# Delta-rule attention and Fourier mixing: combined operands for the first batch, the second weight converted later, constants loaded ahead of memsets

## The chip, the cores and the metric

The kernel runs on one core of one Trainium2 chip. The metric is the device time of one execution in microseconds (us). TensorE (PE in the profile) multiplies matrices, VectorE (DVE) and ScalarE (ACT) do elementwise work, GpSimd (POOL) does a little of it and starts some DMAs, and SyncE (SP) starts most of the DMAs. PEld is TensorE's loading of the stationary operand.

## The reference

The first block is a delta-rule attention with 4 batches, 8 heads, 768 steps and head size 48. The second mixes its output with a two-dimensional Fourier transform, normalises it and sends it through two weight matrices.

```python
# attention, per batch and head
k_n = k / (norm(k) + 1e-6)
for t in range(S):
    y[t] = q[t] @ state
    v_old = state.T @ k_n[t]
    state = state + beta[t] * outer(k_n[t], v[t] - v_old)
# bridge: (B, H, S, D) -> x of (B, S, H*D) = (4, 768, 384)
mixed = real(fft(fft(x, axis=1), axis=2))
u = x + mixed
un = (u - mean(u)) / sqrt(var(u) + 1e-6)
out = u + relu(un @ w_ch1) @ w_ch2          # 384 -> 1536 -> 384
```

Queries, keys, values and beta come as 32-bit floats. The two weights come as 64-bit floats, so the kernel has to make 32-bit words of them itself.

## The kernel before

**Chunks.** The sequence is cut into chunks of 64 steps, 12 a batch and 48 in all; four chunks form a quad, two quads a group. Write K, Q and V for the keys, queries and values of a chunk, S for the state ahead of it, B for beta and the norms, and T for the inverse of a unit triangular 64x64 matrix made of K K^T and B. Then the chunk's contribution is U = T B (V − K S), the next state is S + K^T U, and the output is Q S plus a masked (Q K^T) U. Only S runs from chunk to chunk; everything else can be made ahead.

**Making ahead.** `prepare` (L342 and on) transposes keys and queries on TensorE (`pt`), copies them into the tile KQT (L374, L378, L379), forms the products K K^T and K Q^T (`pg`), copies the first into A (L405, L407) and masks the second into LQ (L410). `squares` (L335, L336) and `norms_of` (L427 to L438) give the norms of the keys. `invert(g)` works on a whole group of two quads: 30 steps of two VectorE instructions each (L463, L465), transposes on VectorE (L448, L472, L474), and two small rounds of matmuls (`pj`) by which the 64x64 inverses come together in the tiles wt (L496 to L500); wt holds T B transposed. `scaled` (L185) scales the values.

**The chain.** `chain(m)` issues chunk m: `pk` = K S on TensorE, R = V − pk on VectorE (L537), `pu` = T B R on TensorE, a copy of it into U on ScalarE (L546), `pS` = K^T U on TensorE, and two sums on VectorE that give the next state (L563). `pk`, `pu` and `pS` all lie in one PSUM tile, which the profile calls pc. `outputs` adds the two parts of the output in `py` and copies them into x (L583), in halves that the next chunk's chain carries along. At the start of each quad, chain asks for more keys, queries and values (SP's DMAs, L156).

**The rest of the work.** When a batch's chunks are done, `second` runs `fourier` on its x (VectorE sums and differences into the scratch tile scr from L624 on, matmuls `pf` and `pb`, sums into x, L660, statistics, L689) and then `mlp`, which takes two row tiles at a time: normalise and transpose (L706, `ptr`, L711), twelve blocks of three matmuls against w1 (`ph`, L723), then the products with w2 (`po`), and the last sum and the store (L736). The tile hT between the two weights has one buffer. A last row group of a batch is left for the batch after it.

**The weights.** `weights` reads each 64-bit weight as pairs of words through a staging tile, in 24 passes: ScalarE makes two pieces (L288, L290), VectorE puts the sign in (L306), shifts (L309) and adds (L312). Each pass uses one of two temporaries, on the tags F and scr, which `fourier` uses too.

**The order.** Each helper is a generator that gives up control after a piece. The loop at the end of the kernel takes the chunks in order and, at each of the three points where `chain` gives up control, advances the work ahead (`pre`) and the work on the side (`side`) by 2.4 pieces each; during the first eight chunks `side` advances only when `pre` is done. `side` is first the weights, and from chunk 12 on, after what is left of the weights has been run, `second` of the batch before. At every eighth chunk what is left of `pre` is run. A planner then places each engine's instructions, in the main by this order, and may move ready instructions ahead of waiting ones[...].

**The start.** POOL first clears tiles (L133), then starts the DMAs for the packed constants (`pack`, which holds the identity for the transposes, L192), beta (`bt`, L194, in a tile on the tag F) and the first key and value rows (L196, L197). The first matmuls are those that turn beta by chunk (`psb`, L124), whose copy is bcol (L224), and after them come the transposes of `keys(0)`.

Of the kernel before, what the change touches and what calls it, by code (L numbers as in the profile page):

```python
# [17 lines left out]
CH = 64  # L18
# [64 lines left out]
def kernel(  # L83
# [46 lines left out]

    def zeroed(shape, name, eng, part=lambda t: t):
        t = const.tile(shape, F32, name=name)
        eng.memset(part(t), 0.0)  # L133
        return t
# [53 lines left out]
    pack = const.tile([128, 128 + CH + NBH + 2], F32, name="pack")  # L188
    bt = wk.tile([NBH, S], F32, tag="F", name="bt")
    k0 = const.tile([NBH, D], F32, name="k0")  # L190
    v0 = const.tile([NBH, D], F32, name="v0")
    nc.gpsimd.dma_start(out=pack, in_=cn["pack"].ap())  # L192
    load(0, 0, (nc.sync, nc.scalar))
    nc.gpsimd.dma_start(out=bt, in_=beta.rearrange("b h s -> (b h) s"))  # L194
    load(1, 0, (nc.sync, nc.scalar))
    nc.gpsimd.dma_start(out=k0, in_=k.rearrange("b h s d -> (b h) s d")[:, 0, :])  # L196
    nc.gpsimd.dma_start(out=v0, in_=v.rearrange("b h s d -> (b h) s d")[:, 0, :])  # L197
# [18 lines left out]


    psb = ps_one([128, NCH, NBH // 2], "psb")
    for n in range(NCH):
        for hh in range(2):  # L220
            t0 = CH * n + (1 if n < NCH // 2 else 0)
            mm(psb[64 * hh:64 * hh + 64, n, :], bt[:, t0:t0 + CH], sel[:, hh, :], n == 0)
    bcol = const.tile([128, B * NQ, QT * 4], F32, name="bcol")
    nc.vector.tensor_copy(bcol.rearrange("p (b i) (c u) -> p b (i c) u", b=B, u=4),  # L224
                          psb.rearrange("p n (b u) -> p b n u", b=B))
    nl = NCH // 2 - 1
    twice = bcol[:, :, 4 * (nl % QT):4 * (nl % QT) + 4].rearrange(
        "p (b i) u -> p b i u", b=B)[:, :, nl // QT]
    nc.vector.tensor_scalar(twice, twice, once, None, op0=ALU.mult)
# [21 lines left out]
    def weights():  # L251

        if moe_w_ch1.dtype == F32:
            nc.sync.dma_start(out=w1, in_=moe_w_ch1.rearrange("(c p) f -> p c f", p=128))
            nc.sync.dma_start(out=w2, in_=moe_w_ch2.rearrange("(c p) m -> p c m", p=128))
            return
        w1v = moe_w_ch1.bitcast(I32).rearrange("(c p) (f two) -> p c f two", p=128, two=2)
        w2v = moe_w_ch2.bitcast(I32).rearrange("(c p) (m two) -> p c m two", p=128, two=2)  # L260
        nw = DFF // 2
        halves = [(w1v[:, i, a * nw:a * nw + nw], w1[:, i, a * nw:a * nw + nw])
                  for i in range(KD) for a in range(2)]
        n2 = nw // DM
        halves += [(w2v[:, i:i + n2], w2[:, i:i + n2]) for i in range(0, KF, n2)]
        stage = wk.tile([128, 2, nw, 2], I32, tag="hT", name="w64")

        def fetched(i):
            if i < len(halves):
                src, t = halves[i][0], stage[:, i % 2]  # L270
                if len(src.shape) == 4:
                    t = t.rearrange("p (c m) two -> p c m two", c=src.shape[1])
                nc.sync.dma_start(out=t, in_=src)

        np_ = nw // 2
        tmps = [wk.tile([128, 2, np_], I32, tag=tag, name="wtmp") for tag in ("F", "scr")]

        def words(p):
            cs = slice(p % 2 * np_, (p % 2 + 1) * np_)
            return stage[:, p // 2 % 2, cs, 0], stage[:, p // 2 % 2, cs, 1], tmps[p % 2]  # L280

        def first(p):

            lo, hi, t = words(p)
            tc.keep_in_program_order(nc.scalar.activation(  # L288
                t[:, 0], lo.bitcast(mybir.dt.uint32), ACT.Copy, scale=2.0 ** -29))
            tc.keep_in_program_order(nc.scalar.activation(  # L290
                t[:, 1].bitcast(F32), hi.bitcast(F32), ACT.Abs, scale=2.0 ** -112))

        fetched(0)
        fetched(1)
        yield
        first(0)
        for p in range(2 * len(halves)):
            lo, hi, t = words(p)
            dst = halves[p // 2][1]
            if len(dst.shape) == 3:  # L300
                dst = dst.rearrange("p c m -> p (c m)")
            dst = dst[:, p % 2 * np_:(p % 2 + 1) * np_].bitcast(I32)
            low, mag = t[:, 0], t[:, 1]
            if p + 1 < 2 * len(halves):
                first(p + 1)
            tc.keep_in_program_order(nc.vector.scalar_tensor_tensor(  # L306
                low, hi, -2 ** 31, low, op0=ALU.bitwise_and, op1=ALU.bitwise_or))
            yield
            tc.keep_in_program_order(nc.vector.tensor_scalar(  # L309
                mag, mag, 3, None, op0=ALU.logical_shift_left))  # L310
            u16 = mybir.dt.uint16
            nc.vector._custom_dve(dve_ops.ADD32_U16LIMBS, out=dst.bitcast(u16),  # L312
                                  in0=mag.bitcast(u16), in1=low.bitcast(u16))
            if p % 2:
                fetched(p // 2 + 2)
            yield
# [21 lines left out]
    def prepare(Q, parts=(0, 1)):  # L338
# [4 lines left out]
        a0, na = parts[0], len(parts)  # L343
        g, lh = divmod(Q, 2)
        if 0 in parts:
# [7 lines left out]
            if Q == NB:  # L353
                KQT = xbufs[2].rearrange("p t d -> p (t d)")[:, 0:QT * 8 * CH].rearrange(
                    "p (c j h a t) -> p c j h a t", c=QT, j=2, h=2, a=2)
            else:
                KQT = wk.tile([128, QT, 2, 2, 2, CH], F32, tag="KQT", bufs=NB, name="KQT")
# [5 lines left out]
        for c2 in range(QT // 2):  # L363
            for c in (2 * c2, 2 * c2 + 1):
                pt = ps_one([128, na, 2, 2, CH], "pt")
                for a in parts:
                    for j in range(2):
                        tr(pt[:, a - a0, j].rearrange("p h t -> p (h t)"),
                           (kp, qp)[a][:, c, 2 * j:2 * j + 2, :].rearrange("p u d -> p (u d)"),
                           a == a0 and j == 0)  # L370
                dst = KQT[:, c, :, :, a0:a0 + na].rearrange("p j h a t -> p a (j h) t")
# [3 lines left out]
                else:  # L375

                    if na == 2:
                        nc.scalar.activation(dst[:, 0], src[:, 0], ACT.Copy)  # L378
                    nc.scalar.activation(dst[:, na - 1], src[:, na - 1, :, ::-1], ACT.Copy)  # L379
# [124 lines left out]

    def chain(m):
# [29 lines left out]
        R = wk.tile([128, 4, D], F32, tag="R", name="R")  # L535
        ue = "p (j e) d -> p e j d"
        nc.vector.tensor_tensor(R.rearrange(ue, e=2), V4[:, c].rearrange(ue, e=2), pk, op=ALU.subtract)  # L537
        yield from advancing(later)

        pu = pc[:, 0, 4 * D:8 * D].rearrange("p (u d) -> p u d", u=4)  # L540
        for u in range(4):
            for hh in range(2):
                pr = slice(64 * hh, 64 * hh + 64)
                mm(pu[pr, u], wt[pr, c, u], R[pr, u], True)
        U = wk.tile([128, 4, D], F32, tag="U", bufs=2, name="U")
        nc.scalar.activation(U, pu, ACT.Copy)  # L546
# [226 lines left out]
    def second(b):  # L773
# [5 lines left out]
        else:  # L779
            yield from fourier(b)  # L780
        yield from mlp(b, list(range(TH if b == B - 1 else TH - 1)))
# [16 lines left out]
    side = weights()  # L798
    advance(side)
    run(keys(0))  # L800
    load(2, 0)
# [10 lines left out]
    scaled(0)  # L812
    pre = both(invert(1), queries(2, 3))
    due = [0.0, 0.0]
    for m in range(STEPS):
        b, n = divmod(m, NCH)
        if m % (2 * QT) == 0 and m > 0:
# [3 lines left out]
            due = [0.0, 0.0]  # L821
        for i, _ in enumerate(chain(m)):
# [51 lines left out]
```

## Time and profile before

| | |
|---|---|
| median of 6 runs | 832.75 us (824.89 to 837.65) |
| profiled execution | 835.15 us |
| its span, first to last instruction | 833.4 us |
| PE busy | 739.7 us, 89% of the span |
| weight load busy | 548.4 us, 66% |
| DVE busy | 398.2 us, 48% |
| ACT busy | 286.0 us, 34% |
| mean granted TensorE clock | 0.903 |
| start of the first Fourier mixing (L624) | 166.9 us |
| start of the first `ph` | 204.5 us |

An instruction's line in the profile is its line in the kernel file; nearly all matmuls come from one helper (L124) and are told apart by the tile that they write. A 32-bit matmul appears as two records for one call in the source, a transpose as one. The durations and idle times are of one execution. The granted clock is the part of full speed that TensorE was given.

### The profile page before, as it was taken

To read this page: it belongs to the slowest core of one execution; us is meant where nothing else is said; L and a number is where in the kernel's file an instruction comes from. 1 tells how busy PE (TensorE), PEld (TensorE's weight loads), DVE (VectorE), ACT (ScalarE), POOL (GpSimd) and SP (SyncE) were. 2 spreads that over 40 slices of the span, in tenths; PEclk is the share of its full clock that TensorE was granted. 3 is DMA by queue.
4 is the path that set the end of the run, shared out by engine and by line. 5 is a ranking of instruction groups with operands and counts; after the bars stand their busy time and mean duration, and the time that the engine had idled before them with its cause. 6 is when DMAs were issued, how large, how long until landed. Compare 5 with 4: busy or idle time off the path is not lost.

```text
span 833.4 us, 18790 instructions
## 1 busy us (share of the span) xinstructions
PE 739.7 (89%) x8024; PEld 548.4 (66%) x8024; DVE 398.2 (48%) x1036; ACT 286.0 (34%) x667; POOL 45.8 (5%) x67
## 2 busy tenths in 40 slices
PE   4768776785999987889999999999899989999997
PEld 3537565674767666665766766766667667676784
DVE  5985968859951146981169313499110124310000
ACT  5725258532273141371431632511521113030120
POOL 3000000011000000010000001000000010000000
PEclk9985955577999996999999699999699999999999
DMA  7542326610111121101102001001000000000000
GB/s 156 119 102 44 62 40 191 181 20 15 26 30 24 36 40 24 20 13 35 28 18 46 2 11 30 1 2 39 2 2 20 2 20 1 9 10 20 9 10 19
DMA packets 84051, 30.81 MB, mean 37 GB/s; under 512 B 79248, under 2 KB 80784, under 8 KB 83968
## 3 DMA queue, kind: packets, MB, share of 16 engines
q1 hardware_dynamic: 80880, 26.63, 14.6%
q0 software_dynamic: 912, 2.59, 0.9%
q8 instruction: 63, 1.03, 0.5%
q10 hardware_dynamic: 2176, 0.39, 0.3%
q14 instruction: 20, 0.16, 0.1%
HBM read 24.87 MB, written 4.72 MB: 36 GB/s over the span
## 4 chain that ended last, share of the span: by engine, by line
PE 70%; DVE 12%; ACT 11%; DMA 3%; issue 3%; SPq 1%; POOL 1%; POOLq 0%; ACTq 0%; DVEq 0%
PE ph L124 22%; PE po L124 21%; PE pc L124 7%; PE py L124 6%; PE pg L124 3%; PE pf L124 3%; PE pj L124 2%; PE pb L124 2%; PE pt L127 2%; DMA w<-in_moe_w_ch_dram 2%; ACT A L407 2%; DVE X L465 1%; ACT wt L497 1%; DVE A L463 1%; DMA kp<-in_k_dram 1%
## 5 line engine op out<-in xcount | busy, mean ns | idle before, releaser
L124 PE MATMUL ph<-unT,w 128*128 128x256 f32 x864 | 222.4, 406 | 6.2 <-ACT hT L723 2.9
L124 PE MATMUL po<-w,hT 128*128 128x384 f32 x576 | 200.3, 495 | 0.0
L124 PEld LDWEIGHTS ph<-unT,w 128*128 128x128 f32 x864 | 164.6, 199 | 37.4 <-ACT hT L723 6.1
L124 PEld LDWEIGHTS po<-w,hT 128*128 128x128 f32 x576 | 105.1, 190 | 65.3 <-issue 0.5
L723 ACT ACTIVATE hT<-ph 128x256 f32<-128x256 f32 x144 | 55.0, 383 | 208.8 <-PE ph L124 208.5
L563 DVE TENSOR_TENSOR st<-st,pc 48x192 f32<-48x192 f32 x88 | 30.9, 351 | 95.8 <-PE pc L124 63.0
L736 DVE TENSOR_TENSOR x<-x,po 128x384 f32<-128x384 f32 x24 | 13.3, 554 | 126.6 <-PE po L124 126.5
L546 ACT ACTIVATE U<-pc 128x192 f32<-128x192 f32 x48 | 15.8, 330 | 120.7 <-PE pc L124 115.7
L124 PE MATMUL pc<-R,wt 64*64 64x48 f32 x768 | 42.4, 249 | 12.3 <-DVE R L537 7.1
L124 PEld LDWEIGHTS pc<-R,wt 64*64 64x64 f32 x768 | 34.3, 160 | 28.0 <-DVE R L537 9.0
L463 DVE TENSOR_TENSOR A<-X 128x30 f32<-128x30 f32 (+9 forms) x150 | 50.6, 337 | 3.8
L465 DVE TENSOR_TENSOR X<-X,A 128x30 f32<-128x30 f32 (+9 forms) x150 | 49.3, 328 | 3.7
L124 PE MATMUL py<-st,KQT 128*64 128x96 f32 x352 | 44.9, 275 | 1.2 <-ACT x L583 1.2
L407 ACT ACTIVATE A<-pg 32x256 f32<-32x256 f32 x108 | 36.6, 369 | 18.4 <-PE pg L124 17.7
L124 PE MATMUL pg<-KQT 48*64 48x128 f32 (+1 forms) x896 | 35.8, 306 | 6.8 <-ACT w L407 2.3
L124 PE MATMUL py<-U,LQ 64*64 64x48 f32 x768 | 40.7, 240 | 0.0
L124 PEld LDWEIGHTS pg<-KQT 48*64 48x64 f32 x896 | 27.8, 173 | 17.8 <-ACT KQT L374 4.7
L124 PEld LDWEIGHTS py<-st,KQT 128*64 128x64 f32 x352 | 34.8, 152 | 5.9 <-ACT x L583 1.9
L124 PEld LDWEIGHTS py<-U,LQ 64*64 64x64 f32 x768 | 34.6, 154 | 2.2 <-issue 1.2
L660 DVE TENSOR_TENSOR x<-x,pb 128x193 f32<-128x193 f32 (+1 forms) x96 | 27.1, 345 | 18.3 <-PE pb L124 18.3
L124 PE MATMUL pf<-stab,scr 128*128 128x128 f32 (+6 forms) x192 | 27.6, 294 | 9.1 <-DVE scr L634 8.9
L583 ACT ACTIVATE x<-py 64x384 f32<-64x384 f32 x44 | 21.3, 484 | 38.5 <-PE py L124 37.1
(127 smaller groups left out, 811.5 us busy)
## 6 DMA issues: line engine op xcount, KB each, us to landing
w<-in_moe_w_ch_dram SPq DMA_DIRECT2D x12, 768.0 KB, 5.2
qp<-in_q_dram SPq DMA_DIRECT2D x96, 48.0 KB, 2.6
V<-in_v_dram SPq DMA_DIRECT2D x96, 48.0 KB, 2.5
kp<-in_k_dram SPq DMA_DIRECT2D x88, 48.0 KB, 2.4
out_dram<-x SPq DMA_DIRECT2D x8, 192.0 KB, 1.9
out_dram<-x SPq DMA_DIRECT2D x4, 168.0 KB, 2.1
stab<-k_stab SPq DMA_DIRECT2D x1, 640.5 KB, 4.3
kp<-in_k_dram ACTq DMA_DIRECT2D x8, 48.0 KB, 3.4
```

What stands on the lines that cost most here:

```text
L124: nc.tensor.matmul(o, lhsT=lhsT, rhs=rhs, start=start, stop=stop, skip_group_check=True)
L127: nc.tensor.matmul(o, lhsT=src, rhs=ident[0:src.shape[0], 0:src.shape[0]], is_transpose=True, start=start, stop=True, skip_group_check=True)
L407: nc.scalar.activation(ce(A[pr, ns, :, sl]), src, ACT.Copy)
L463: nc.vector.tensor_tensor(t, X[:, j:j + 1, j + 1:].broadcast_to([128, j, n]), X[:, 0:j, j:j + 1].broadcast_to([128, j, n]), op=ALU.mult)
L465: nc.vector.tensor_tensor(X[:, 0:j, j + 1:], X[:, 0:j, j + 1:], t, op=ALU.add)
L497: nc.scalar.activation(wt[r1, :, :, 0:W], Z[r1, ns], ACT.Copy)
L546: nc.scalar.activation(U, pu, ACT.Copy)
L563: nc.vector.tensor_tensor(nst[pr, :, :, e, :], st[pr, :, :, e, :], pS[pr], op=ALU.add)
L583: nc.scalar.activation(xs[b][yr, T].rearrange("p (h u d) -> p h u d", h=2, u=4), py[yr], ACT.Copy, scale=live[yr] if n == NCH // 2 - 1 els ...
L660: nc.vector.tensor_tensor(dst, dst, src, op=op)
L723: nc.scalar.activation(hT[:, fc, :], ph, ACT.Relu)
L736: nc.vector.tensor_tensor(x[:, T, :], x[:, T, :], po, op=ALU.add)
```

## The change

Three things change.

First, in batch 0 (chunks 0 to 11) the chain no longer multiplies by T B. A new function, `combined(m)`, forms T B K transposed (`pm`) and T B V (`pv`) for a chunk and writes them over the keys in KQT and over the values. The chain's R is then U itself. `combined` is called two chunks ahead inside the chain; for chunks 0, 1, 8 and 9 it is called in front of the chain. Because quad 3 belongs to batch 1 and its KQT lay in a buffer that now has another use, its keys are transposed once more into a usual KQT tile together with its queries.

Second, `weights` takes a part. Part 0, the first weight, stands where both stood. Part 1, the second weight, is staged in the third x buffer in three slots; its first fetches start at chunk 12, and its twelve passes come one behind each of the first `ph` blocks of batch 0.

Third, the four POOL DMAs for constants, beta and first rows are issued ahead of the tile clearing, and the beta matmuls move behind `keys(0)`.

```diff
+    pack = const.tile([128, 128 + CH + NBH + 2], F32, name="pack")
+    bt = wk.tile([NBH, S], F32, tag="F", name="bt")
...
+    nc.gpsimd.dma_start(out=pack, in_=cn["pack"].ap())
+    nc.gpsimd.dma_start(out=bt, in_=beta.rearrange("b h s -> (b h) s"))
+    nc.gpsimd.dma_start(out=k0, in_=k.rearrange("b h s d -> (b h) s d")[:, 0, :])
+    nc.gpsimd.dma_start(out=v0, in_=v.rearrange("b h s d -> (b h) s d")[:, 0, :])
...
     def zeroed(shape, name, eng, part=lambda t: t):
...
-    psb = ps_one([128, NCH, NBH // 2], "psb")
-    for n in range(NCH):
...
+    def betas():
+
+        psb = ps_one([128, NCH, NBH // 2], "psb")
...
-    def weights():
+    def weights(part):
...
-        stage = wk.tile([128, 2, nw, 2], I32, tag="hT", name="w64")
+        np_ = nw // 2
+        if part == 0:
+            halves = [(w1v[:, i, a * nw:a * nw + nw], w1[:, i, a * nw:a * nw + nw])
+                      for i in range(KD) for a in range(2)]
+            n, stage = 2, wk.tile([128, 2, nw, 2], I32, tag="hT", name="w64")
+        else:
+            halves = [(w2v[:, i, a * np_:a * np_ + np_], w2[:, i, a * np_:a * np_ + np_])
+                      for i in range(KF) for a in range(DM // np_)]
+            n, stage = 1, xbufs[2].rearrange("p t d -> p (t d)")[:, 0:6 * np_].bitcast(I32).rearrange(
+                "p (i f two) -> p i f two", i=3, two=2)
+        ns = stage.shape[1]
...
-        fetched(0)
-        fetched(1)
-        yield
+        for i in range(ns):
+            fetched(i)
+        yield
+        tmps = [wk.tile([128, 2, np_], I32, tag=tag, name="wtmp") for tag in ("F", "scr")]
         first(0)
...
+        again = Q == NB and parts == (1,)
+        taken = (0, 1) if again else parts
...
             if Q == NB:
-                KQT = xbufs[2].rearrange("p t d -> p (t d)")[:, 0:QT * 8 * CH].rearrange(
+                KQT = w2.rearrange("p c m -> p (c m)")[:, 2048:2048 + QT * 8 * CH].rearrange(
                     "p (c j h a t) -> p c j h a t", c=QT, j=2, h=2, a=2)
-            else:
-                KQT = wk.tile([128, QT, 2, 2, 2, CH], F32, tag="KQT", bufs=NB, name="KQT")
+        if Q != NB and 0 in parts or again:
+            KQT = wk.tile([128, QT, 2, 2, 2, CH], F32, tag="KQT", bufs=NB, name="KQT")
...
+    def combined(m):
+
+
+        Q, c = divmod(m, QT)
+        KQT, kp, _ = held[Q]
+        wt = wts[Q % NB]
+        scaled(Q)
+        pm = ps_pair("pm", "pair")[:, :, 0:2 * CH].rearrange("p h (j t) -> p h j t", j=2)
+        for j in range(2):
+            for hh, e in ((0, 0), (1, 1), (0, 1), (1, 0)):
+                pr = slice(64 * hh, 64 * hh + 64)
+                mm(pm[64 * e:64 * e + 64, hh, j], kp[pr, c, 2 * j + e, :], wt[pr, c, 2 * j + e], j == 0)
+        nc.scalar.activation(KQT[:, c, :, :, 0, :].rearrange("p j h t -> p h j t"), pm, ACT.Copy)
+        pv = ps_one([128, 4, D], "pv")
+        for u in range(4):
+            for hh in range(2):
+                pr = slice(64 * hh, 64 * hh + 64)
+                mm(pv[pr, u], wt[pr, c, u], vals[Q][pr, c, u], True)
+        nc.scalar.activation(vals[Q][:, c], pv, ACT.Copy)
+
     def chain(m):
...
-        R = wk.tile([128, 4, D], F32, tag="R", name="R")
+        if m < NCH:
+            U = R = wk.tile([128, 4, D], F32, tag="U", bufs=2, name="U")
+        else:
+            R = wk.tile([128, 4, D], F32, tag="R", name="R")
...
+        if m < NCH:
+            if (m + 2) % (2 * QT) > 1 and m + 2 < NCH:
+                combined(m + 2)
+        else:
+
+            pu = pc[:, 0, 4 * D:8 * D].rearrange("p (u d) -> p u d", u=4)
...
         else:
+            w = weights(1)
+            advance(w)
             yield from fourier(b)
-        yield from mlp(b, list(range(TH if b == B - 1 else TH - 1)))
+        channels = mlp(b, list(range(TH if b == B - 1 else TH - 1)))
+        if b == 0:
+            for _ in range(KF + 1):
+                advance(channels)
+                advance(w, 2)
+                yield
+            run(w)
+        yield from channels
...
-    side = weights()
+    side = weights(0)
     advance(side)
     run(keys(0))
+    betas()
...
-    scaled(0)
+    combined(0)
+    combined(1)
     pre = both(invert(1), queries(2, 3))
...
+            for i in (m, m + 1):
+                if i < NCH:
+                    combined(i)
```

## The prediction

> **What bounds the kernel now.** The profiled execution took 835.15 us for a span of 833.4 us. I read the busy time of each engine by stage first (columns: stretch in us, its length, busy us and instruction count of PE, weight load, DVE, ACT, POOL, granted TensorE clock, DMA share, GB/s).
>
> ```profile
> 0.00:69.30 69.30, 43.10 (x654) 31.25 (x654) 50.84 (x139) 38.77 (x94) 9.78 (x19) 0.92 0.56 119
> 69.30:121.30 52.00, 41.88 (x948) 35.79 (x948) 39.58 (x98) 18.51 (x39) 0.00 (x0) 0.70 0.28 46
> 121.30:158.00 36.70, 25.80 (x492) 22.63 (x494) 29.80 (x70) 27.95 (x63) 0.00 (x0) 0.50 0.61 184
> 158.00:167.00 9.00, 7.86 (x126) 6.94 (x124) 7.60 (x25) 4.57 (x12) 0.00 (x0) 0.50 0.53 133
> 167.00:204.50 37.50, 26.29 (x255) 20.74 (x251) 28.03 (x80) 12.17 (x31) 6.77 (x9) 0.77 0.11 19
> 204.50:233.00 28.50, 28.12 (x236) 21.76 (x235) 26.32 (x65) 7.88 (x19) 0.00 (x0) 0.94 0.11 19
> 250.00:302.00 52.00, 52.00 (x493) 36.52 (x488) 7.05 (x17) 13.03 (x34) 1.53 (x2) 1.00 0.15 30
> ```
>
> From 204.5 us, where the first channel matmuls (ph) begin, to the end PE is busy 594.8 of 628.9 us: that part is PE's, and the change adds no matmul to it. Before it PE is busy 144.9 of 204.5 us, half of the time at half clock. So the change is worth what it moves the start of ph, less what it stalls PE afterwards.
>
> What fixes the start of ph? The time order of DVE and ACT around 160 us (start, duration, instruction):
>
> ```profile
> 157.54 0.48 ACT L583 ACTIVATE x<-py 64x384 f32<-64x384 f32 x1 [1.62 <-PE py L124]
> ...
> 164.20 0.55 DVE L306 SCALAR_TENSOR_TENSOR wtmp<-w,wtmp 128x384 int32<-128x384 int32 x1
> 164.67 0.35 DVE L309 TENSOR_SCALAR wtmp<-wtmp 128x384 int32<-128x384 int32 x1
> ...
> 165.06 0.56 DVE L312 CUSTOM_DVE_ANT_0 w<-wtmp 128x768 uint16<-128x768 uint16 x1
> 166.66 0.35 DVE L563 TENSOR_TENSOR st<-st,pc 48x192 f32<-48x192 f32 x1 [1.05 <-PE pc L124]
> 166.94 1.34 DVE L624 TENSOR_TENSOR scr<-x 128x1152 f32<-128x1152 f32 x1
> ```
>
> The last output of batch 0 is in x at 158.0; the Fourier mixing (L624) begins only at 166.9, behind the weight conversion, which ends at 165.6 and also holds the scratch buffers (tags F and scr). The sizes, from the groups:
>
> ```profile
> L312 DVE CUSTOM_DVE_ANT_0 w<-wtmp 128x768 uint16<-128x768 uint16 x24 | 13.6, 566 | 0.2
> L306 DVE SCALAR_TENSOR_TENSOR wtmp<-w,wtmp 128x384 int32<-128x384 int32 x24 | 13.3, 553 | 5.7 <-ACT wtmp L288 5.5
> L288 ACT ACTIVATE wtmp<-w 128x384 int32<-128x384 uint32 x24 | 13.1, 544 | 3.4 <-DMA w<-in_moe_w_ch_dram 2.5 <-DVE w L312 0.7
> L290 ACT ACTIVATE wtmp<-w 128x384 f32<-128x384 f32 x24 | 12.9, 539 | 0.0
> L546 ACT ACTIVATE U<-pc 128x192 f32<-128x192 f32 x48 | 15.8, 330 | 120.7 <-PE pc L124 115.7
> ```
>
> **The change, part by part.** One conversion pass is .553 + .353 (L309) + .566 = 1.47 us of DVE and 1.08 of ACT. By the starts of L306, 3 of the 24 passes run before 121.3, 17 from there to 158.0 and 4 after.
>
> *Second weight moved.* 12 passes (17.7 us DVE, 13.0 us ACT) leave the front. The other 12 keep their place: 3 early, 9 after 121.3. So the stretch 121.3–158.0 loses 8 passes: DVE 29.8 − 11.8 = 18.0, ACT 27.95 − 8.6 = 19.3. The 9.0 us behind it (4 passes) stops standing between x and L624.
>
> *Combined operands.* Per chunk of batch 0, 8 source matmuls (pu; 16 records) and the copy U (.33) go; 8 for pm, 8 for pv (32 records), a copy into KQT (128x256, .38 as L374 and L379 take) and one into V (128x192, .33) come. Sixteen pc<-R records took 1.09 us at half clock (154.12) and .67 at full clock (88.55). Pm's 64 columns I put at 1.2 or .75; so a chunk costs PE 1.2 or .75 us more. Here the Trainium skill (TensorE: Matmul & The Clock Gate, table "Why this matters for your kernels") speaks of the clock: without idle gaps over about 3 us TensorE should keep full speed. The trace disagrees: from 145.0 to 177.2 us the granted clock is half, though no PE gap exceeds 1.5 us. By the rule the stretch 121.3–158.0 would hold about (25.8 + 4.8) × .62 = 19 us of PE work; by the row, 25.8 + 4 × 1.2 = 30.6 us. I take the row. That makes PE the largest sum there (DVE 18.0, ACT 19.3 + 4 × .38 = 20.8), and with 2.4 us of dependency gaps (10.9 us of PE idle there today, most of it behind conversion instructions) it becomes 33.0 us: 3.7 earlier. Together with the 9.0 us: 12.7 us for the start of L624.
>
> In 69.3–121.3 the shorter chain buys little. One step there takes PE .45 + .87 + .67 + .40 + .65 = 3.0 us at full clock and recurs after 4.2 to 5.0 (R at 83.96, 88.12, 93.14, 97.65), while invert(1) keeps DVE at 17.0 of 20 us in 80–100. The wait R→pu→U goes (about .9 us a step beyond PE's work), .75 of PE work comes; the end of invert(1), which gives wt of quad 2, is set by DVE. At chunk 0 the combination is serial behind wt (pm, copy, pk, R instead of pu, U: +2 us). The repeated K transposes of quad 3 are 8 records of about .3 us, 2.4 us of PE, among PE idle of 10 us. Bounds: 2 us earlier, 4 later; I take 0, the value of the DVE row.
>
> *Constants first.* Pack's DMA is issued at 4.18, behind 3.5 us of POOL memsets; psb waits until 8.82 for beta and holds the first transposes until 11.5. Key data were there at 6.5. The first KQT copy (12.22) may come 1 to 3 us sooner; ACT's table loads and squares (to 10.95) hold it. Against this, psb's 2.7 us of PE comes after keys(0), and the temporary on tag F, which bt occupies, is free later: passes 0 and 1 slide from 18–23 us toward invert(0), which starts at 26.4; at worst their 2.9 us of DVE are lost there. Bounds: 2.5 gain, 2 loss; I take 1 us gain, nearest to ACT's 10.95 against 12.22.
>
> *What becomes late next.* Chunks 12 and 13, done beside the last passes today, now lie beside the mixing. 167.0–204.5 has PE 26.3 and DVE 28.0 of 37.5 us; 7.9 us of PE and 7.6 − 5.9 = 1.7 of DVE join. It fits; bounds 0 and 7, I take 2 us lost.
>
> *Where the second weight lands.* Thirteen side steps of the first group: each has one ph block (6 records, 1.54 us), one pass, one step of invert(2) (.66) and .15 of the chain on DVE: 2.28 us of DVE against about 1.96 of PE (with the chain). Twelve passes end after 27 us; po begins after about 24 us and wants its last piece of w2 some 7 us later, so po itself isn't held. But DVE stands at 26.3 of 28.5 us in 204.5–233, so invert(2) ends up to 17.7 us later, and wt of quad 4 with it (238.4 today). PE can go on with po (about 17 us) and the next ph (18.5); DVE is idle 45 of 52 us after 250, where the backlog drains. Queued behind a pass on DVE are R and the state sums, on ACT the hT copies: an hT copy may start 1.08 us late against 1.54 us per ph. SP's queue gets 12 fetches of 384 KB, each waiting for its pass; the key, query and value loads behind them have a quad's time. Bounds 0 and 15.5 (17.7 less 2.2 of idle in that stretch); I take 2 us, nearest to the idle row 250–302.
>
> **Sum.** 12.7 + 0 + 1 − 2 − 2 = 9.7 us off the profiled 835.15: 825.5. The median of the runs is 2.4 below that execution: 823.1, said as 823. A difference within 1% (8.3 us) can't be told from no change.
>
> **The rivals.**
> *A, this forecast* (40%): 815–829, median 823.
> *B, the clock rises* (20%): 0.96 granted in 80–100, half from 102; the denser PE work of 121–158 keeps full clock, 19 us of work plus gaps makes 24 instead of 33: 9 more, 814. Against it: the stretch without gaps at half clock.
> *C, PE takes it back* (15%): at half clock the added 12 × 1.2 = 14.4 us of PE lies on the path in 69–158 instead of in its gaps (R→pu→U wasn't the bound, PE was); 823 + 10: 833. The change then doesn't shorten the chain it is written for.
> *D, the backlog comes due* (25%), the slower case: the DVE queue delays wt of quad 4 beyond the PE work that may pass it. Its price is 15.5 us instead of 2 at 204–250, and as batch 1's steps are then without side work, half as much again (8) around 302–344, where PE is idle 8.3 of 42 us today: 823 + 13.5 + 8 = 845. It decides once more than about 11.7 us of PE idle appears between the first ph and 300 us.
>
> **How the numbers follow.** Faster by over 1% is below 824.4: B whole, .28 of A: .48. Within 1%: the rest of A (.12) and C (.15), with .01 of D: .28. Slower, above 841.1: .24. The range cuts the outer part of B and of D: 808 to 843.
>
> **What would show it.** Right: L624 some 12 to 14 us earlier, first ph likewise, passes of w2 between the ph blocks, PE still about 28 of the 28.5 us after the first ph. Wrong: R steps in 78–108 spaced wider than 5 us, PE idle at po or at pc<-R of chunk 16, a granted clock of half there, or 121–158 not shorter although the passes are gone.

## The result, and the profile after

The changed kernel takes 831.66 us (median of 34 runs, 821.02 to 842.75), the kernel before 833.11 us (71 runs, 824.89 to 844.89). The ratio is 0.9955 with a 95% interval of 0.9936 to 0.9974: about 3.7 us faster, 2.1 to 5.3. The ratio leaves disturbed executions of both kernels out, so that it is not the quotient of the two medians. The direction was forecast, and the time lies in the range (808 to 843), but the gain is 3.7 us where the sum said 9.7, and it is within the 1% that was called no change.

First the busy time by stage of the changed kernel, in the same stretches and columns as before:

```profile
0.00:69.30 69.30, 32.79 (x598) 25.67 (x600) 50.66 (x136) 34.88 (x85) 10.08 (x19) 1.00 0.58 128
69.30:121.30 52.00, 44.40 (x1038) 38.08 (x1034) 38.32 (x96) 20.96 (x45) 0.00 (x0) 0.88 0.23 38
121.30:158.00 36.70, 32.92 (x655) 27.68 (x652) 24.21 (x61) 25.69 (x61) 1.27 (x1) 0.59 0.42 103
158.00:167.00 9.00, 8.61 (x127) 7.86 (x120) 5.26 (x12) 1.71 (x4) 1.59 (x2) 0.70 0.32 54
167.00:204.50 37.50, 29.59 (x302) 22.67 (x301) 30.70 (x88) 17.71 (x46) 3.31 (x6) 0.86 0.24 56
204.50:233.00 28.50, 28.42 (x187) 19.76 (x187) 26.54 (x75) 13.20 (x31) 0.00 (x0) 1.00 0.44 112
250.00:302.00 52.00, 51.22 (x639) 37.04 (x639) 14.12 (x36) 19.48 (x53) 2.28 (x2) 1.00 0.19 36
```

In the third row PE is busy 32.9 of 36.7 us (25.8 before). The passes have gone to the sixth row, where DVE has 26.5 of 28.5 us and PE is nearly always busy. The time order of ACT and DVE around the end of batch 0 shows what the move of the second weight was to bring:

```profile
159.99 0.47 ACT L619 ACTIVATE x<-py 64x384 f32<-64x384 f32 x1
160.49 1.36 DVE L660 TENSOR_TENSOR scr<-x 128x1152 f32<-128x1152 f32 x1 [1.92 <-ACT x L619]
```

The mixing (now L660) begins 0.5 us after the last output's copy into x begins; before it was 9.4 us (157.54 to 166.94). But that copy begins at 160.0 and not at 157.5, although eight passes have left its stretch. By the groups of the changed kernel, the passes are the same 24, only elsewhere (L317: 24 with a mean of 553 ns, 566 before), and the copies of U are 36 instead of 48.

TensorE's order around chunk 8, where the second group of two quads begins, shows where the chain now stands:

```profile
122.78 0.66 PE L124 MATMUL pv<-V,wt 64*64 64x48 f32 x4 [1.26 <-ACT wt L508]
123.40 0.70 PE L124 MATMUL pm<-wt,kp 64*64 64x64 f32 x16
...
125.48 1.92 PE L124 MATMUL pj<-Z,w 32*32 32x32 f32 x64
...
130.85 1.92 PE L124 MATMUL pj<-w 32*32 32x32 f32 x64
...
135.19 0.71 PE L124 MATMUL pm<-wt,kp 64*64 64x64 f32 x16
...
137.06 0.40 PE L124 MATMUL pc<-st,KQT 48*64 48x48 f32 x16
```

Seven chunks' pm (112 records) lie before 116 us, so the pm at 123.40 is chunk 7's and the one at 135.19 chunk 8's. The pv at 122.78 is already chunk 8's: it starts behind the copy into wt (L508) that it waits for. pm of chunk 8 reads the same wt and waits 12 us more. In between lie the two rounds of `pj` for quad 3 (125.48 and 130.85), which chunk 8 does not need.

The two profiled executions differ by 9.1 us of span (824.3 against 833.4), more than the timed difference. The same changed kernel profiled again has 836.5 us; so a single span could not have given the verdict. The early time marks repeat well: the last copy of batch 0 into x begins at 160.0 and 160.7 us.

The marks that the experiments use, from one profile of each kernel (us; "R8" is chunk 8's R, which is U itself where the operands are combined):

| kernel | inverse 0 starts | R1 | R8 | R11 | last copy into x | first mixing | first ph |
|---|---|---|---|---|---|---|---|
| before | 26.4 | 77.9 | 116.8 | 153.7 | 157.5 | 166.9 | 204.5 |
| after | 29.3 | 87.3 | 138.1 | 155.9 | 160.0 | 160.5 | 196.8 |
| after, again | 29.1 | 87.1 | 138.4 | 156.6 | 160.7 | 161.2 | 199.5 |
| weights only | 25.8 | 77.4 | 121.7 | 150.0 | 155.6 | 156.1 | 194.5 |
| weights and early DMAs | 27.0 | 77.0 | 118.8 | 146.9 | 152.5 | 153.0 | 191.8 |
| weights and constants | 29.3 | 79.9 | 123.6 | 151.9 | 155.5 | 156.0 | 194.0 |
| combined only | 26.6 | 85.0 | 134.8 | 159.5 | 163.8 | 175.7 | 212.7 |

R8 alone makes the delay look larger than it is: without the combination the chain passes chunk 8 early and stands at chunk 9 instead. R9 is at 136.1 us before, at 134.2 with the weights alone, and at 143.1 after.

### The profile page after: what moved, and what is told of

The parts are those of the page before. It is cut to its first block, busy times and chain, and to the rows that moved or that the text cites. A ratio compares the mean times of both kernels' runs of the same rounds, so it can differ in the third digit from the quotient of the medians.

```text
span 824.3 us, 19211 instructions
## 1 busy us (share of the span) xinstructions
PE 731.9 (89%) x8224; PEld 544.0 (66%) x8224; DVE 397.1 (48%) x1036; ACT 289.5 (35%) x679; POOL 45.6 (6%) x67
## 4 chain that ended last, share of the span: by engine, by line
PE 69%; DVE 13%; ACT 11%; issue 3%; DMA 2%; SPq 1%; POOL 0%; ACTq 0%; POOLq 0%; DVEq 0%
PE po L124 22%; PE ph L124 20%; PE py L124 6%; PE pc L124 5%; PE pg L124 3%; PE pj L124 3%; PE pf L124 3%; DVE X L474 2%; PE pb L124 2%; PE pt L127 2%; DVE A L472 2%; ACT wt L506 2%; ACT A L416 2%; ACT wt L509 1%; DVE Z L481 1%
## 5 line engine op out<-in xcount | busy, mean ns | idle before, releaser
L124 PEld LDWEIGHTS ph<-unT,w 128*128 128x128 f32 x864 | 161.6, 196 | 36.7 <-ACT hT L759 6.5
L582 ACT ACTIVATE U<-pc 128x192 f32<-128x192 f32 x36 | 11.9, 331 | 112.3 <-PE pc L124 97.5
L124 PE MATMUL py<-st,KQT 128*64 128x96 f32 x384 | 49.2, 275 | 2.3 <-ACT x L619 2.3
L124 PEld LDWEIGHTS py<-st,KQT 128*64 128x64 f32 x384 | 38.0, 152 | 9.5 <-ACT x L619 4.2
L416 ACT ACTIVATE A<-pg 32x256 f32<-32x256 f32 x108 | 36.7, 369 | 19.5 <-PE pg L124 17.4
L124 PE MATMUL py<-U,LQ 64*64 64x48 f32 x768 | 42.4, 238 | 0.0
L124 PE MATMUL pc<-R,wt 64*64 64x48 f32 x576 | 29.6, 237 | 11.3 <-DVE R L569 7.6
L124 PEld LDWEIGHTS pc<-R,wt 64*64 64x64 f32 x576 | 23.6, 147 | 24.2 <-DVE R L569 8.6
L639 POOL DMA_INDIRECT out_dram<-x,rows_hi x12 | 12.2, 1013 | 412.2 <-DVE x L772 195.1
```

The costliest lines, as they stand in the source:

```text
L124: nc.tensor.matmul(o, lhsT=lhsT, rhs=rhs, start=start, stop=stop, skip_group_check=True)
L416: nc.scalar.activation(ce(A[pr, ns, :, sl]), src, ACT.Copy)
L639: nc.gpsimd.indirect_dma_start(out=out.rearrange("b s m -> (b s) m"), out_offset=bass.IndirectOffsetOnAxis(ap=rows_hi[:, i:i + 1], axis=0) ...
```

## The experiments

My theory after the result: moving the second weight brings all of the gain, and the combined operands give a part of it back before batch 0's output is complete. The rivals: the constants cost it (the first inverse starts 3 us later), the passes at their new place cost it, or the late `pm` of chunk 7 costs it. One more rival, the granted clock behind chunk 8, had no experiment of its own; what the traces say of it stands with the kernel combined from chunk 2 on.

### Each part alone

**Only the second weight moved.** The changed kernel with the combination switched off and the start as before:

```diff
-        if m < NCH:
+        if m < 0:
             U = R = wk.tile([128, 4, D], F32, tag="U", bufs=2, name="U")
...
-    combined(0)
-    combined(1)
+    scaled(0)
...
-    nc.gpsimd.dma_start(out=pack, in_=cn["pack"].ap())    # and the three others: behind the memsets
...
     run(keys(0))
-    betas()                                                # ahead of keys(0)
```

> Only the second weight is moved; the chain and the start are those of before. Theory 1 (the combined operands and the late beta matmuls hold the front back, and take away what the weight move gives): L624-type mixing starts at 150 to 156 us instead of 166.9, and the whole is 7 to 11 us faster than before, so faster than the full change. Theory 2 (the weight move only shifts VectorE work to where it costs the same, and the gain measured is that of the shorter chain): within 2 us of before.

Measured: 824.79 us, ratio 0.9915 (0.9877 to 0.9952), so 7.1 us faster than before (4.0 to 10.2). The time order of ACT and DVE at the end of batch 0 in this kernel, and its stage from 121.3 to 158.0 us (columns as above):

```profile
155.61 0.47 ACT L621 ACTIVATE x<-py 64x384 f32<-64x384 f32 x1
156.11 1.36 DVE L662 TENSOR_TENSOR scr<-x 128x1152 f32<-128x1152 f32 x1 [1.75 <-ACT x L621]
```

```profile
121.30:158.00 36.70, 31.17 (x558) 27.17 (x554) 25.25 (x62) 22.90 (x53) 1.71 (x2) 0.50 0.37 94
```

The copy is 1.9 us earlier than before and the wait of 9 us is gone as well; the mixing starts at 156.1 us, at the edge of what was expected. The first ph comes 10.0 us earlier. The stage runs at half clock throughout, and is still the quicker one. That this kernel is faster than the full change is not shown: the intervals overlap.

**Only the combined operands.** The kernel before with `combined` and its calls, nothing else:

```diff
+        if m < NCH:
+            U = R = wk.tile([128, 4, D], F32, tag="U", bufs=2, name="U")
+        else:
             R = wk.tile([128, 4, D], F32, tag="R", name="R")
...
-    scaled(0)
+    combined(0)
+    combined(1)
```

> Only the combined operands; both weights are converted in front as before. Theory 1: chunk 0's U comes 8 us later, the chunks after it 1 to 1.5 us apart less, the end of batch 0 at about the same time; with the conversion still ahead of the mixing the whole is 0 to 5 us slower than before. Theory 2: 3 to 6 us faster.

Measured: 841.64 us, ratio 1.0149 (1.0091 to 1.0206): 12.4 us slower, more than either theory expected. The same view of this kernel (ACT's copy, the last pass of the weights, the mixing):

```profile
163.78 0.47 ACT L610 ACTIVATE x<-py 64x384 f32<-64x384 f32 x1
...
175.10 0.56 DVE L312 CUSTOM_DVE_ANT_0 w<-wtmp 128x768 uint16<-128x768 uint16 x1
...
175.69 1.36 DVE L651 TENSOR_TENSOR scr<-x 128x1152 f32<-128x1152 f32 x1
```

The chain is 6.2 us later at its end, and with the passes still in front the mixing waits for the last of them: 8.8 us later than before. The first ph is 8.2 us later; the other 4 us of the timed loss I have not traced.

**The changed kernel again,** unchanged, on the same chip as the two above.

> The full change once more, beside the parts on the same chip. Both theories: 2 to 6 us faster than before. Its profile tells how far one profiled execution stands for the others: the pair so far is 9.1 us apart in span where the medians are 1.5 to 4 us apart; if that difference is the clock granted to one execution, this profile's span is 826 to 832.

Measured: 829.36 us, 0.9951 (0.9911 to 0.9990), which agrees with the result. Its span (836.5; 826 to 832 was expected) is 12.2 us above the first profile's; 2.7 of that is there at the first ph, and 9.1 lie between the second and the third Fourier mixing. There TensorE was granted half clock in the second profile and full clock in the first. The rows of those stretches, the changed kernel's second profile and then its first:

```profile
360.00:381.00 21.00, 20.57 (x302) 16.14 (x296) 11.44 (x35) 9.54 (x25) 2.20 (x3) 0.51 0.06 12
```

```profile
355.00:380.00 25.00, 23.86 (x425) 17.00 (x426) 13.63 (x41) 11.33 (x28) 2.20 (x3) 1.00 0.10 20
```

This is why the experiments are judged by timed ratios and by marks ahead of 200 us.

**All but the combination:** second weight and constants. Of the edit of the first experiment only this part, with DMAs and `betas` as changed:

```diff
-        if m < NCH:
+        if m < 0:
```

> The full change without the combined operands: second weight moved, constants first, beta matmuls behind the first keys. Theory 1: 2 to 6 us faster than the full change. Theory 2: 3 to 6 us slower than the full change, so about as before.

Measured: 827.43 us, ratio 1.0001 (0.9958 to 1.0043). Its runs spread from 824.8 to 840.0 us, and the median (4.8 us below the 832.24 us of before) and the ratio say different things. The 2 to 6 us below the changed kernel that my theory expected did not show: by the medians it is 1.9 us faster than the changed kernel on this chip (829.36), by the ratios slower (1.0001 against 0.9951), and the intervals overlap. So by time it is not shown that the combination costs anything here. The marks, of one execution, are on the theory's side: the first inverse starts 3.5 us later than in the kernel with the weights alone, as in the changed kernel, but the last copy into x begins at 155.5 against 155.6 us and the first ph at 194.0 against 194.5. So of the constants nothing is left at the first ph, and the 4.5 us from 155.5 to 160.0 go with the combination, the one difference between the two kernels.

### Where the second weight stands

**Neither here nor there.** Two kernels that leave the second weight's twelve passes out and load queries into w2 in their stead: the changed kernel without them (first cut) and the kernel before without them (second cut; the load of queries stands there too, further down).

```diff
-            w = weights(1)
-            advance(w)
+            nc.sync.dma_start(out=..., in_=...)   # queries into w2
```

```diff
-        halves += [(w2v[:, i:i + n2], w2[:, i:i + n2]) for i in range(0, KF, n2)]
```

> The full change without the conversion of the second weight: its twelve passes and their fetches are left out, and part of the queries is loaded into the second weight's tile in their place, so the output differs. It prices what the passes cost where they have landed. If they are hidden there (forecast's 2 us, or less): first ph to the end within 2 us of the full change's 622.6 us of span. If the backlog comes due: 10 to 20 us shorter.

> The kernel before with the twelve passes of the second weight left out in the same way. It prices what they cost where they stood. Both theories: the first mixing starts at 153 to 157 us instead of 166.9, the whole is 7 to 12 us faster than before, about as the weights-only kernel.

Measured: the changed kernel without the passes 827.0 us, 0.9921 (0.9884 to 0.9958), the kernel before without them 820.95 us, 0.9858 (0.9812 to 0.9904). So the passes cost 11.8 us (8.0 to 15.7) where they stood, and about 2.8 us (0.9955 less 0.9921) where they now stand; the second figure is not clear of zero, since the two intervals together leave it between −0.6 and 6.3 us. The time order at the end of batch 0 in the kernel before without the passes:

```profile
156.42 0.47 ACT L582 ACTIVATE x<-py 64x384 f32<-64x384 f32 x1
156.92 1.36 DVE L623 TENSOR_TENSOR scr<-x 128x1152 f32<-128x1152 f32 x1 [1.97 <-ACT x L582]
```

and the stage after the first ph in the changed kernel without them:

```profile
204.50:233.00 28.50, 26.78 (x309) 19.61 (x307) 20.85 (x49) 12.60 (x26) 0.00 (x0) 1.00 0.13 22
```

Without the passes the copy into x begins at 156.4, only 1.1 us earlier than before: the 8 passes that lie beside the chain cost it little, and nearly the whole price was the wait behind them. At the new place DVE is busy 20.9 us of that stage without the passes and 26.5 with them, and with them PE is idle for 0.1 us of it. From the first ph to the second mixing it takes 115.8 us without the passes and 118.8 and 119.2 with them, so 3.0 to 3.4 us. The span from the first ph to the end, which the expectation names, decides nothing: 631.6 us without the passes, 627.5 and 637.0 in the two profiles of the changed kernel (the expectation's 622.6 is not what the first profile gives).

**Weights and the early DMAs,** without the combination, the beta matmuls in their old place:

```diff
     run(keys(0))
-    betas()
...
+    betas()
```

> Second weight moved and the four constant loads ahead of the memsets, but the beta matmuls ahead of the keys as before and no combined operands. Theory (the beta matmuls behind the first keys cost the first inverse 2.6 to 3.5 us, the early loads gain 1 to 3): first inverse starts (X transpose) at 23 to 25 us instead of 25.8 in the weights-only kernel and 29.3 in the kernel with all of the constants' part; whole 1 to 3 us below weights-only. Rival (the start doesn't matter because ScalarE's ladder sets it): X transpose at 25.5 or later, whole as weights-only.

Measured: 827.44 us, 0.9892 (0.9837 to 0.9947), not to be told from the weights alone (0.9877 to 0.9952). The first inverse starts at 27.0 us, 2.3 earlier than with the beta matmuls moved (29.3), but 1.2 later than with the weights alone (25.8); 23 to 25 was expected, so at the inverse the early loads gained nothing. By the marks the last copy into x (152.5) and the first ph (191.8) are 3.1 and 2.7 us earlier than with the weights alone; by the times this is not shown. Of the 3.5 us by which the first inverse was late, 2.3 go with `betas` behind `keys(0)`. TensorE in the changed kernel, at 16 us:

```profile
16.54 2.74 PE L124 MATMUL psb<-pack,bt 32*64 32x16 f32 x48
19.21 0.69 PE L127 MATMUL pt<-pack,kp 128*128 128x128 f32 x2
```

The 2.7 us of psb now stand between transposes that the inverse needs.

### What holds the combined chain

**pm out of the shared PSUM tile.** In the code `pm` and the inverse's `pj` lie in PSUM tiles of the same tag, "pair", which has one buffer; that this holds the chain is theory 1a of the expectation below. Here pm takes two tiles of the other tag, "one", which has two buffers:

```diff
-        pm = ps_pair("pm", "pair")[:, :, 0:2 * CH].rearrange("p h (j t) -> p h j t", j=2)
+        pm = [ps_one([128, 2, CH], "pm") for _ in range(2)]
...
-        nc.scalar.activation(KQT[:, c, :, :, 0, :].rearrange("p j h t -> p h j t"), pm, ACT.Copy)
+        for hh in range(2):
+            nc.scalar.activation(KQT[:, c, :, hh, 0, :], pm[hh], ACT.Copy)
```

> The full change, but the product pm is formed in two single PSUM tiles (tag one, two copies into KQT) instead of the one-buffer PSUM pair that the inverse's matmuls and the key products also use. Theory 1a (the combined operands of chunk 7 stand behind the inverse of the next group because they share that one buffer): chunk 7's R starts at 112 to 116 us instead of 128, batch 0's last copy into x at 150 to 155 instead of 160, whole 4 to 9 us below the full change. Theory 1b (the late start of chunk 0 and the added TensorE work set it): R of chunk 7 at 120 or later, whole within 2 us of the full change.

Measured: 836.92 us, 1.0058 (1.0017 to 1.0099): slower than the kernel before, where a gain was expected. R7 came at 122.2 us (128.1 in the changed kernel; 112 to 116 expected), the last copy into x at 162.8. TensorE at chunk 8 in this kernel (eight chunks' pm, 128 records, lie before 116 us, so this is chunk 8's):

```profile
126.53 0.36 PE L124 MATMUL pm<-wt,kp 64*64 64x64 f32 x1
...
127.31 1.92 PE L124 MATMUL pj<-Z,w 32*32 32x32 f32 x64
129.16 0.69 PE L124 MATMUL pm<-wt,kp 64*64 64x64 f32 x8
...
132.28 0.98 PE L124 MATMUL pv<-V,wt 64*64 64x48 f32 x13 [0.64 <-ACT KQT L527]
...
133.75 1.92 PE L124 MATMUL pj<-w 32*32 32x32 f32 x64
...
136.01 0.67 PE L124 MATMUL pc<-st,KQT 48*64 48x48 f32 x12
```

pm of chunk 8 now starts at 126.5, 8.7 us earlier, and before both rounds of pj for quad 3 (127.31 and 133.75): so the shared tile was what had held it. But the chain gets only 1.3 us of it (R8 at 136.8 against 138.1). pm holds both tiles of the tag "one" until its copies, so pv waits for them; the copies (131.95) stand behind conversion copies on ScalarE; and pk stands behind a round of pj and chunk 9's pm in TensorE's list. One wait was replaced by three smaller ones. From R8 to the last copy into x this kernel then takes 26.0 us, the changed one 21.9, and by the ratios it is some 9 us slower as a whole; why is open.

**Combination from chunk 2 on,** chunks 0 and 1 in the old form:

```diff
-        if m < NCH:
+        if m in (2, 3, 4, 5, 6, 7, 8, 9, 10, 11):
...
-    combined(0)
-    combined(1)
+    scaled(0)
```

> The full change, but chunks 0 and 1 keep the old form (T B applied in the chain); chunks 2 to 11 are combined. If the late start of chunk 0 (second R at 87 instead of 78 to 80) is what the combination costs, R of chunk 1 is at 79 to 81, the last copy into x of batch 0 at 152 to 155 instead of 160, and the whole is 4 to 8 us below the full change. If it isn't, because a later chunk waits for the inverse anyway, chunk 8's R stays at 136 or later and the whole within 2 us of the full change.

Measured: 827.96 us, 0.9924 (0.9877 to 0.9972). R1 is at 81.3 instead of 87.3, but R8 is at 139.8: the six microseconds are lost again at chunk 8. From R9 to the last copy into x it then took 10.7 us (145.7 to 156.4), against 16.9 in the changed kernel (143.1 to 160.0). The rows of these two stretches, the changed kernel's and then this one's:

```profile
143.09:159.99 16.90, 16.06 (x236) 12.94 (x236) 8.86 (x26) 6.05 (x19) 1.27 (x1) 0.50 0.28 48
```

```profile
145.68:156.38 10.70, 8.77 (x196) 7.13 (x194) 7.38 (x25) 4.44 (x13) 1.26 (x1) 0.86 0.32 56
```

In the changed kernel PE is busy for 95% of the stretch, at half clock; the 32 records of one `pg` there take 1.99 us (147.64), here 1.10 (148.48). So a chunk 8 that comes as late as in the changed kernel need not end the batch as late: with the higher clock, and somewhat fewer records, the last copy is back at 156.4. What gave one kernel the higher clock is open. The first ph (197.1) is the changed kernel's.

**Combination at chunks 8 to 11 only,** on the kernel with the weights alone:

```diff
-        if m < NCH:
+        if m in (8, 9, 10, 11):
```

> The second weight moved, start and chunks 0 to 7 as before, combined operands for chunks 8 to 11 alone. If the short chain pays where nothing hides it (17.8 us from chunk 8's R to chunk 11's in the full change, 28.3 without it), batch 0's last copy into x is at 147 to 152 instead of 155.6, and the whole is 2 to 6 us below weights-only, so the best of all. If what it saves is spent in front of chunk 8 (pm, copy, state product behind the inverse), the last copy is at 155 or later and the whole as weights-only or slower.

Measured: 829.6 us, 0.9970 (0.9930 to 1.0011); against 0.9915 for the weights alone, with overlapping intervals. TensorE at chunk 8 in this kernel (there is no pm before it), and then in the kernel with the weights alone:

```profile
124.26 0.66 PE L124 MATMUL pv<-V,wt 64*64 64x48 f32 x4 [0.79 <-ACT wt L510]
...
131.43 1.92 PE L124 MATMUL pj<-w 32*32 32x32 f32 x64
...
134.96 0.71 PE L124 MATMUL pm<-wt,kp 64*64 64x64 f32 x16
```

```profile
124.46 1.08 PE L124 MATMUL pc<-R,wt 64*64 64x48 f32 x14
127.64 0.57 PE L124 MATMUL pc<-U,kp 64*48 64x48 f32 x16 [0.69 <-ACT U L584]
```

Here the price of the wait stands by itself. pv reads chunk 8's wt at 124.3, as pu does in the old form at 124.5, so wt was there; pm follows 10.7 us later, after the last pj. R8 moves from 121.7 to 137.3. Afterwards the chain catches up (R9 to R11 in 8.7 us instead of 15.8), and the last copy into x is at 156.2 against 155.6. The combination gets back what it lost, no more. Even that is not the short chain's alone: from R9 to the last copy the granted clock is 0.92 here and 0.50 in the kernel with the weights alone.

**Chunk 7 in the old form,** all else as changed:

```diff
-        if m < NCH:
+        if m in (0, 1, 2, 3, 4, 5, 6, 8, 9, 10, 11):
```

> The full change, but chunk 7 keeps the old form. If chunk 7's product, placed behind the inverse of the next group, is the cost, chunk 7's R is at 113 to 117 instead of 128, chunk 8's at 126 to 132 instead of 138, and the whole 3 to 7 us below the full change. If the start of chunk 0 is, chunk 8's R stays within 3 us of 138 and the whole within 2 us of the full change.

Measured: 834.37 us, 1.0039 (1.0007 to 1.0072). R7 comes at 114.4 instead of 128.1 us, but R8 stays at 138.8, and the last copy into x is even later (163.0). So the late pm of chunk 7, my rival cause, is not what sets R8: chunk 8 is late by its own pm. Why this kernel is slower than the changed one is open.

**Chunks 2 to 6 only,** on the kernel with the weights alone:

```diff
-        if m < NCH:
+        if m in (2, 3, 4, 5, 6):
```

> The second weight moved, start as before, combined operands for chunks 2 to 6 alone, the chunks that run beside VectorE's steps of the next inverse. If VectorE sets the end of that stretch and the shorter chain buys nothing there, the inverse's transpose Z of group 1 starts at 111 to 115 us as in weights-only (111.6), batch 0's last copy into x is at 154 to 158 (155.6), and the whole is within 3 us of weights-only. If the added TensorE work costs there, Z is 3 or more later and the last copy too; if the shorter chain frees VectorE, Z is before 109.

Measured: 827.65 us, 0.9949 (0.9912 to 0.9985). This leaves out chunks 0 and 1, chunk 7, and chunks 8 and 9, where the combination had to wait. The transpose Z begins at 115.1 us, 3.5 later than with the weights alone (111.6), which is the sign named for TensorE work that costs; but the kernel combined at chunks 8 to 11 only, which changes nothing ahead of chunk 8, has it at 115.8, so the sign decides nothing. R8 (114.8) is the earliest of all, but R9 (138.95) is later than with the weights alone (134.2), and the last copy into x is at 156.5 against 155.6. So even here the time that the combination saves ahead of chunk 8 does not reach the end of the batch.

## Why the prediction was right or wrong

| step of the sum | forecast | measured |
|---|---|---|
| passes no longer between x and L624 | 9.0 earlier | 8.9 (wait 9.4 to 0.5) |
| 121.3–158.0 becomes 33.0, 0 for 69.3–121.3, constants first: last copy into x | 3.7 + 0 + 1 = 4.7 earlier | 2.5 to 3.2 later |
| chunks 12, 13 beside the mixing | 2 lost | 1.3 gained and 0.7 lost (two profiles: 36.3 and 38.3 us, 37.6 before) |
| second weight at its new place | 2 lost | 2.8 by time (−0.6 to 6.3), 3.0 to 3.4 by marks |

The first ph was to come 11.7 us earlier and comes 7.7 and 5.0 earlier in the two profiles. The end of batch 0 missed its forecast by 7.2 and 7.9 us; that the mixing lost less than the 2 us put down for it covered a part of this.

**Right: the weight.** What fixed the start of the first mixing was the conversion, and taking it away gave what was read from the two lines around 158 and 167 us. Alone it is worth 7.1 us (4.0 to 10.2).

**Wrong: "it becomes 33.0 us: 3.7 earlier", and the 0 for the stretch ahead of it.** The last copy into x was to come 4.7 us earlier. It comes 1.9 to 5.0 earlier in the three kernels without the combination, and 2.5 to 3.2 later in the changed one. The step took the largest busy sum of the stretch, PE's 30.6 us, and put on 2.4 us of gaps, as if the chain entered the stretch at the same chunk as before. It does not: R7 and R8 lay at 107.8 and 116.8 us before, ahead of 121.3, and lie at 128.1 and 138.1 in the changed kernel. Their work falls into the stretch as well:

```profile
121.30:160.00 38.70, 34.84 (x685) 29.44 (x680) 24.56 (x62) 25.93 (x63) 1.27 (x1) 0.59 0.42 101
```

PE is busy 34.8 us here in place of 30.6, and idle 3.9 in place of 2.4: 38.7 us where 33.0 were forecast. The cost of pm is not the reason, since its 16 records take 0.71 us at half clock and 0.46 at full clock, where 1.2 and 0.75 were put down. The reason is the order: at the start of the second group chunk 8 can begin only when its pm is through, and pm stood behind quad 3's share of the inverse until 135.2 us. Chunk 7 waited for its own pm too, until 123.4 us; in the old form its R is at 114.4. The prediction named such a serial piece for chunk 0 (2 us; R1 is in fact 7.3 us later than in the kernel with weights and constants alone) and overlooked that chunks 8 and 9 are called in front of the chain in the same way, and that pm shares a PSUM tag with pj. The place of pm in the queue for a shared buffer cost chunk 8 a wait of 12 us, its work 0.7.

How much of the end at 160.0 us is this wait is shown only in part. At the same half clock, the changed kernel's R9 is 8.9 us later than with the weights alone and 4.5 of that are won back by the last copy into x. Two kernels whose R8 is about as late (139.8 and 137.3) end at 156.4 and 156.2, with a granted clock of 0.86 and 0.92 behind R9 in place of 0.50. The runs do not separate the wait from the clock.

**"I take 0" for 69.3 to 121.3** held for the inverse: its transpose Z comes at 114.4 us, 2.7 later than before, after a start that was 2.9 later. It did not hold for the chain, which leaves the stretch with R6 done and not R8. In the middle the chain does run faster (R2 to R5 every 3.0 us, before 4.2 to 5.0). What goes with each place of the combination, chunks 0 and 1, 2 to 7, 8 to 11, the timed intervals do not separate; they overlap. By the marks, no place gains at the last copy into x.

**Constants.** The first KQT copy came 0.9 us earlier (11.28 against 12.22), as forecast, though the kernel with the weights alone, whose start is that of before, has it at 11.64. The loss on the other side was 2.9 us at the first inverse, beyond the bound of 2 us. Neither is left at the first ph.

**The clock.** From 121.3 to 158.0 the granted clock was 0.59, with PE busy 90% of the stretch. The row of before (0.50) was the better guide; full clock would have made 19 us of the PE work, and 32.9 were measured. The row that the prediction set against the rule of 3 us, from 145.0 us on, was not a good test of it: a gap of 3.5 us on PE (141.5 to 145.0) ends just there. The changed kernel is a better one. Its clock, at 1.00 since 137 us, falls to 0.50 at 143 us and stays there until past 162 us. PE's longest gap between 120 and 160 us is 1.7 us (141.8 to 143.5), and behind it PE is busy 16.1 of 16.9 us. In rival B's first stretch, 69.3 to 121.3, the clock did rise, from 0.70 to 0.88; in the second it did not.

**The rivals.** C is near in time (833 against 831.7), and it is not refuted: PE is busy 34.8 of 38.7 us up to the last copy, so PE work lies on the path there. But at most 8.5 us of it (12 times 0.71) are pm's, not 14.4; and what delays chunk 8 is the place of its pm in the order and in the shared buffer, since on other tiles it started 8.7 us sooner. D did not come: from the first ph to 300 us PE is idle for 3.1 us, where 11.7 were to decide for it. Of the signs named for a wrong forecast the stretch 121–158 came, which is not shorter although eight passes have left it. R steps wider than 5 us came too (6.0 us twice, from 81.2 to 93.3), but the kernel before has one as wide (77.9 to 84.0). That the time still lies in the range is owed to the width of the range, which took in C.

**A better version.** The second weight moved, without the combination, is faster than the kernel before (0.9915, and 0.9892 with the early DMAs), by medians also than the changed one (824.79 against 829.36 us on the same chip). But the intervals overlap with the changed kernel's 0.9936 to 0.9974, and the third such kernel, with the constants as changed, has 1.0001. So that it beats the changed kernel is likely and not shown.

## What to carry to other kernels

When work is moved from inside a serial chain to ahead of it, look at the chain's starting points: there nothing is ahead, and the new work stands in the queue for its operands, its PSUM buffer and its engine. A sum of busy times is a lower bound for such a stretch, and it holds only for the work that was there before; ask which steps of the chain will fall into it, and follow one step through the wait that ends last. And where work stands in the way of something else, as the conversion stood in front of the mixing, leave it out altogether in a trial: that gives the most that moving it can bring.

## What the runs showed that I had not expected

The granted clock at 355 to 381 us differs between executions of one kernel: 1.00 in the first profile of the changed kernel, 0.51 in the second, in a stretch in which PE was busy 20.6 of 21.0 us. Of the profiles here six of fourteen have it. It goes with 9 us between the second and the third mixing. In the second profile no gap on PE exceeds 0.9 us between 345 us and the fall at 360. What sets it off is open.
